# Gated mix of an S4 convolution and a gated linear unit: three sums of a table on GpSimd in halves, their factors and h in PSUM

## The chip, the cores and the metric

One core of a Trainium2 chip runs the whole program. The metric is device time of one execution, in microseconds (us); the figure for a kernel is the median of its runs. The engines are TensorE (PE, with its weight loads as PEld), VectorE (DVE), ScalarE (ACT), GpSimd (POOL) and SyncE (SP), which issues the DMAs here.

## The reference

With x of 2048 rows (time) and 512 channels, the output is `g * a + (1 - g) * b`:

```
g = sigmoid((x * gate_w).sum(-1))                 # one number a row
# a: S4 convolution, one kernel of 2048 taps a channel d, over 128 complex states n
P = exp(dt * A * l)                               # l = 0 .. 2047
K = einsum("dn,dnl,dn->dl", C, P, dt * B).real
a = irfft(rfft(x, 4096) * rfft(K, 4096))[:2048] + x * Dskip
# b: gated linear unit with 1792 hidden columns
b = (sigmoid(x @ w_gate) * (x @ w_up)) @ w_down
```

All of it is in float32.

## The kernel before

The convolution is done as a transform in two stages, with matmuls against constant matrices. `rows` (L382) transforms x in 16 pieces: load of a piece `u` (buffer tag `xs`, two buffers), four matmuls into two PSUM banks (L390), a copy of one bank by ACT (L391) and of the other by DVE (L392), and two DMAs to DRAM (`a_u`, L394).

`kgen` (L192) makes the taps K in 16 groups of 32 channels. The powers z^l of a state are built as a table `T` in three parts of 32 entries: T[:, 0] holds the small powers times the factor of the state, T[:, 1] powers with the step 32, T[:, 2] continues T[:, 1]. `bases` (L148) makes 11 powers z^(2^k) per group (`bz`) by Exp and Sin on ACT with DVE around it, in scratch tiles of tag `tmp`. `double` (L181) then makes twice as many entries out of those there are, as a complex product: two DVE products, L188 into a `tmp` tile and L189 into the table, and a DVE sum of both, L190. There are six doublings a group, of 64, 256, 512, 1024, 2048 and 2048 elements per partition. 128 small matmuls (L221) multiply the parts of the table and sum over the states into a bank of tag "kg"; ACT copies it (`kst`, L224, two buffers), 32 matmuls (L231) transform it into banks of tag "fft", and ACT puts it into `kev` (L235). T has one buffer: the table of the next group begins when the matmuls of L221 are through.

The gated unit (`glu`, L329) runs beside this. `load_x` (L330) loads half a stretch of x through the `xs` buffers and splits it into a rounded part and the rest. `weights` (L396) does the same with the weights of one block of 128 hidden columns, on DVE at L407 and L408 in the first half, from DRAM in the second. `hidden` (L416) makes 24 matmuls of 512 columns for a block, 12 into a bank for the gate and 12 into one for the up part (tag "gu", three banks). ACT takes the sigmoid (L431), DVE multiplies (`h`, L432), ACT rounds (`hh`, L433), DVE takes the rest (`hl`, L434). After three or four blocks the down products follow (L367, tag "dn", two banks) and a sum on DVE (L373).

After `kgen`, `finish` (L251) multiplies both transforms and goes back in 16 steps; `final` (L313) ends the transform and mixes. They take their banks from "fft" and "kg" as well, and the rest of the gated unit is spread between them.

The program is written in one order: the first table, 24 units of the gated unit, the rows with 32 units after each four, then after each half group 50 units (`run_b`; a unit is one matmul of 512 columns). A planner puts the instructions of each engine into a fixed order by their place in the program, when their inputs and buffers are there in its own account; what stands in `high_priority` (L215 to L239: from L221 to L238) goes first. Each engine works through its list in order, and so does SP with the DMAs. A bank or buffer goes to a new tile when the last reader of the old one is through. PSUM has eight banks: two of "fft", one of "kg", three of "gu" and two of "dn".

## Time and profile before

| | |
|---|---|
| median of 3 runs | 760.19 us (758.28 to 763.95) |
| the profiled execution's own time | 766.59 us |
| its span, first to last instruction | 764.7 us |
| busy share of PE, DVE, ACT, POOL | 93%, 81%, 50%, 0% |
| mean granted clock of TensorE | 0.966 |
| the chain that ended last | PE 44%, DVE 24%, ACT 14%, DMA 12% |

Busy time is the time in which an engine has an instruction in work; matmuls are pipelined, so a busy PE is not PE at its peak. The chain is followed back from the last instruction, at each step to what released it. A group's line has engine, operation, tiles out<-in, shapes and count, then busy us, mean ns of one, and idle time of the engine before them with what ended it. A wait's line has who waited for whom: us in total, times, and the longest.

### The profile page before, as it was taken

What the parts mean: (1) busy time and instruction counts of PE and PEld (TensorE: products, weight loads), DVE (VectorE), ACT (ScalarE), POOL (GpSimd) and SP (SyncE); (2) the same over time, 40 slices, a digit from 0 to 9 for tenths busy, and PEclk for the clock granted to TensorE, in tenths of its full rate; (3) what the DMA queues carried; (4) which work ended last, traced back from release to release, by engine and by line L of the source; (5) the groups of instructions that cost most, each with busy time, mean ns of one, the idle gap of its engine ahead of it and who ended that gap; (6) DMA issues with size and microseconds to landing.
All of it is one profiled execution on the core that took longest, in us unless ns stands there. A gap on an engine that the chain in (4) does not pass through costs nothing.

```text
span 764.7 us, 12698 instructions
## 1 busy us (share of the span) xinstructions
PE 709.3 (93%) x5024; PEld 478.7 (63%) x5024; DVE 622.5 (81%) x851; ACT 379.6 (50%) x624; POOL 3.6 (0%) x36
## 2 busy tenths in 40 slices
PE   5978869999999999999899998999999999999994
PEld 3445437787878778877687786877873333333640
DVE  5889796989998999998999898999927576477452
ACT  5264536381845446374565734637135655656310
POOL 0000000000000000000000000000000000000000
PEclk9789959999999999999999999999999999999998
DMA  6667652353134033655014330423167787876497
GB/s 230 185 201 215 171 158 77 128 188 132 63 110 140 34 132 109 220 172 188 12 34 157 122 150 8 138 96 99 56 244 255 266 264 240 266 249 227 143 308 249
DMA packets 63323, 123.03 MB, mean 161 GB/s; under 512 B 8480, under 2 KB 23072, under 8 KB 62240
## 3 DMA queue, kind: packets, MB, share of 16 engines
q1 hardware_dynamic: 63264, 122.23, 48.6%
q8 instruction: 39, 0.64, 0.3%
q14 instruction: 20, 0.16, 0.1%
HBM read 79.74 MB, written 42.47 MB: 160 GB/s over the span
## 4 chain that ended last, share of the span: by engine, by line
PE 44%; DVE 24%; ACT 14%; DMA 12%; issue 5%; SPq 1%; DVEq 0%; ACTq 0%
PE gups L424 13%; PE dps L367 11%; PE fps L247 8%; DVE T L189 5%; DVE T L190 5%; DVE tmp L188 4%; DMA wst<-wgu 4%; PE ips L280 4%; PE kps L221 3%; ACT L431 2%; PE fps L390 2%; DMA b_in<-b_s 2%; PE fps L231 2%; ACT gu L404 2%; DVE h L432 2%
## 5 line engine op out<-in xcount | busy, mean ns | idle before, releaser
L424 PE MATMUL gups<-xh,gu 128*128 128x512 f32 x896 | 294.5, 404 | 12.7 <-ACT gu L404 10.3
L424 PEld LDWEIGHTS gups<-xh,gu 128*128 128x128 f32 x896 | 170.6, 192 | 66.0 <-issue 12.9
L424 PE MATMUL gups<-xl,gu 128*128 128x512 f32 x448 | 181.3, 405 | 0.0
L367 PE MATMUL dps<-dnw,hh 128*128 128x512 f32 x448 | 152.9, 406 | 11.2 <-ACT hh L433 11.2
L188 DVE TENSOR_TENSOR tmp<-T,bz 128x64 f32<-128x64 f32 (+2 forms) x96 | 114.8, 1196 | 2.4
L190 DVE TENSOR_TENSOR T<-T,tmp 128x64 f32<-128x64 f32 (+2 forms) x96 | 114.7, 1195 | 0.8
L367 PEld LDWEIGHTS dps<-dnw,hh 128*128 128x128 f32 x448 | 84.3, 191 | 49.6 <-ACT hh L433 16.9
L189 DVE TENSOR_TENSOR T<-T,bz 128x64 f32<-128x64 f32 (+2 forms) x96 | 114.7, 1195 | 0.0
L424 PEld LDWEIGHTS gups<-xl,gu 128*128 128x128 f32 x448 | 86.2, 192 | 28.2 <-issue 10.5
L367 PE MATMUL dps<-dnw,hl 128*128 128x512 f32 x224 | 90.1, 404 | 2.1 <-DVE hl L434 1.3
L433 ACT ACTIVATE hh<-h 128x512 fp32r<-128x512 f32 x56 | 35.1, 628 | 70.1 <-DVE h L432 70.1
L431 ACT ACTIVATE sg<-gups 128x512 f32<-128x512 f32 x56 | 33.4, 596 | 50.5 <-PE gups L424 50.1
L367 PEld LDWEIGHTS dps<-dnw,hl 128*128 128x128 f32 x224 | 42.9, 192 | 15.8 <-issue 4.2
L432 DVE TENSOR_TENSOR h<-gups,sg 128x512 f32<-128x512 f32 x56 | 38.2, 685 | 16.9 <-PE gups L424 14.3
L404 ACT ACTIVATE gu<-wst 128x1024 fp32r<-128x1024 f32 x28 | 29.6, 1058 | 41.8 <-DMA wst<-wgu 29.2
L267 DVE TENSOR_TENSOR t<-fps,uf 128x512 f32<-128x512 f32 x32 | 22.0, 687 | 31.2 <-PE fps L247 19.8
L434 DVE TENSOR_TENSOR hl<-h,hh 128x512 fp32r<-128x512 f32 x56 | 38.4, 687 | 9.4 <-ACT hh L433 9.2
L247 PE MATMUL fps<-ak,w_in 128*64 128x512 f32 x128 | 42.1, 610 | 0.1
L235 ACT ACTIVATE kev<-fps 128x256 f32<-128x256 f32 x64 | 33.7, 675 | 15.3 <-PE fps L231 15.3
L247 PE MATMUL fps<-au,w_in 128*64 128x512 f32 x128 | 38.4, 610 | 1.9 <-DVE ud L301 0.8
L373 DVE TENSOR_TENSOR acc<-acc,dps 128x512 f32<-128x512 f32 x48 | 32.2, 682 | 7.8 <-PE dps L367 7.7
L221 PEld LDWEIGHTS kps<-T 128*32 128x32 f32 x2048 | 31.6, 115 | 8.8 <-issue 8.8
(84 smaller groups left out, 691.1 us busy)
## 6 DMA issues: line engine op xcount, KB each, us to landing
wst<-wgu SPq DMA_DIRECT2D x28, 512.0 KB, 4.4
a_u<-evu SPq DMA_DIRECT2D x32, 256.0 KB, 3.3
a_k<-kev SPq DMA_DIRECT2D x8, 1024.0 KB, 6.1
au<-a_u SPq DMA_DIRECT2D x16, 512.0 KB, 5.6
ak<-a_k SPq DMA_DIRECT2D x16, 512.0 KB, 5.0
b_s<-evb SPq DMA_DIRECT2D x32, 256.0 KB, 2.5
b_in<-b_s SPq DMA_DIRECT2D x16, 512.0 KB, 4.7
wsd<-wdn SPq DMA_DIRECT2D x28, 256.0 KB, 3.3
```

The source lines that it names most:

```text
L188: nc.vector.tensor_tensor(t2, src, sb, op=OP.mult)
L189: nc.vector.tensor_tensor(dst, src, br, op=OP.mult)
L190: nc.vector.tensor_tensor(dst, dst, t2[:, :, ::-1], op=OP.add)
L221: mm(p[32 * j:32 * j + 32, s].rearrange("p (a b) -> p a b", a=2), T[:, 0, ch, c], T[:, 1:3, ch, c], start=(c == 0), stop=(c == 1), tile_po ...
L247: mm(p[64 * kb:64 * kb + 64], w[:, kb, 64 * c:64 * c + 64], a(kb), start=True, stop=True, tile_position=(0, 64 * kb), skip_group_check=True)
L367: mm(p, a[:, hs], dnw[:, b], start=(n == 0), stop=(n == last))
L404: nc.scalar.activation(gu[:, 0], s4, AF.Copy)
L424: mm(p, gu[:, a, k, dc], b[:, dc], start=(n == 0), stop=(n == 11))
L431: nc.scalar.activation(sg, pp[0], AF.Sigmoid)
L432: nc.vector.tensor_tensor(h, pp[1], sg, op=OP.mult)
L433: nc.scalar.activation(hh, h, AF.Copy)
L434: nc.vector.tensor_tensor(hl, h, hh.bitcast(F32), op=OP.subtract)
```

## The change

- The sum of the doublings of 1024, 2048 and 2048 elements goes from DVE to GpSimd. Each of these doublings is cut into two calls of `double`: the first two by the parts T[:, 1] and T[:, 0], in this order, the last by its channels, 16 and 16. The scratch tiles have 1024 elements instead of 2048, and there are four instead of two; `bases` takes three tiles instead of one.
- The five powers that these doublings multiply by (and their negatives) are copied by ACT into a PSUM bank `kz`, from which DVE's products read them.
- `h` has no tile in SBUF: DVE's product is written over the up part, in its bank of tag "gu", where ACT and DVE read it.
- `kz` takes a PSUM bank, and the two of "fft" become one "f0". Where a second bank was used, it is "kg" (`rows`, `kgen`) or the one of `kz` (`stage2`, `final`).

```diff
--- before.py
+++ after.py
@@ -35,6 +35,7 @@
 NG = 16
 KS = [6, 0, 7, 1, 8, 2, 9, 3, 10, 4, 5]
 NB = len(KS)
+NZ = 6
 GROUPS = [4, 4, 3, 3]
 HALF = L // 2
 LN2H, LN2L = 0.693145751953125, 1.42860682030941723212e-6
@@ -97,8 +98,8 @@
     bp = ctx.enter_context(pool("bp"))
     ps = ctx.enter_context(pool("ps", 1, PSUM))
 
-    def fps(tag="fft", bufs=2):
-        return ps.tile([P, 512], F32, tag=tag, bufs=bufs, name="fps")
+    def fps(tag):
+        return ps.tile([P, 512], F32, tag=tag, name="fps")
 
 
     wu = cst.tile([P, 2, P], F32, name="wu")
@@ -143,7 +144,7 @@
 
 
     def tmp(pp):
-        return pp.tile([P, 2048], F32, tag="tmp", bufs=2, name="tmp")
+        return pp.tile([P, 1024], F32, tag="tmp", bufs=4, name="tmp")
 
     def bases(pp, gi):
 
@@ -155,10 +156,9 @@
         aa = pp.tile([P, 2, 32], F32, name="aa")
         nc.vector.tensor_tensor(aa, pg[:, 0:2], dg, op=OP.mult)
         sh = [P, 2, NB, 32]
-        t = tmp(pp)
         m = NB * 32
-        th, sc = (t[:, 2 * m * a:2 * m * (a + 1)].rearrange("p (c k b) -> p c k b", c=2, k=NB) for a in range(2))
-        af = t[:, 4 * m:5 * m].rearrange("p (k b) -> p k b", k=NB)
+        th, sc = (tmp(pp)[:, :2 * m].rearrange("p (c k b) -> p c k b", c=2, k=NB) for _ in range(2))
+        af = tmp(pp)[:, :m].rearrange("p (k b) -> p k b", k=NB)
         n = af.bitcast(I32)
         nc.vector.tensor_tensor(th, aa[:, :, None, :].to_broadcast(sh), pw[:, :, :, None].to_broadcast(sh), op=OP.mult)
         nc.scalar.activation(n, th[:, 1], AF.Copy)
@@ -178,16 +178,15 @@
         nc.vector.tensor_tensor(w[:, 1], w[:, 2], cb(1), op=OP.mult)
         return bz, w
 
-    def double(pp, dst, src, bz, k, nd, e):
+    def double(pp, dst, src, b, nd, e, add):
 
         sh = [P, nd, 2, e]
-        b = bz[:, :, k:k + nd // 32].rearrange("p u k b -> p u (k b)")
         t2 = tmp(pp)[:, :2 * nd * e].rearrange("p (d c e) -> p d c e", c=2, d=nd)
         br = b[:, 0, :, None, None].to_broadcast(sh)
         sb = b[:, 1:3].rearrange("p u d -> p d u")[:, :, :, None].to_broadcast(sh)
         nc.vector.tensor_tensor(t2, src, sb, op=OP.mult)
         nc.vector.tensor_tensor(dst, src, br, op=OP.mult)
-        nc.vector.tensor_tensor(dst, dst, t2[:, :, ::-1], op=OP.add)
+        add.tensor_tensor(dst, dst, t2[:, :, ::-1], op=OP.add)
 
     def kgen(pp):
         nxt = bases(pp, 0)
@@ -203,15 +202,24 @@
             nc.gpsimd.memset(T[:, 1, :, 0, 0:1], 1.0)
             nc.gpsimd.memset(T[:, 1, :, 1, 0:1], 0.0)
             nc.scalar.activation(T[:, 1, :, :, 1].rearrange("p d c -> p c d"), bz[:, 0:2, 1], AF.Copy)
-            double(pp, T[:, 0, :, :, 1:2], T[:, 0, :, :, 0:1], bz, 0, 32, 1)
+
+            kz = ps.tile([P, 3, NB - NZ, 32], F32, tag="kz", name="kz")
+            nc.scalar.activation(kz, bz[:, :, NZ:], AF.Copy)
+            double(pp, T[:, 0, :, :, 1:2], T[:, 0, :, :, 0:1], bz[:, :, 0], 32, 1, nc.vector)
             T2 = T[:, 0:2].rearrange("p t d c e -> p (t d) c e")
             for k in range(1, 5):
                 e = 2 ** k
-                double(pp, T2[:, :, :, e:2 * e], T2[:, :, :, 0:e], bz, 2 * k, 64, e)
+                if 2 * k < NZ:
+                    b = bz[:, :, 2 * k:2 * k + 2].rearrange("p u k b -> p u (k b)")
+                    double(pp, T2[:, :, :, e:2 * e], T2[:, :, :, 0:e], b, 64, e, nc.vector)
+                else:
+                    for t in (1, 0):
+                        double(pp, T[:, t, :, :, e:2 * e], T[:, t, :, :, 0:e], kz[:, :, 2 * k + t - NZ], 32, e, nc.gpsimd)
             yield 1
             if gi + 1 < NG:
                 nxt = bases(pp, gi + 1)
-            double(pp, T[:, 2], T[:, 1], bz, 10, 32, 32)
+            for d in (slice(0, 16), slice(16, 32)):
+                double(pp, T[:, 2, d], T[:, 1, d], kz[:, :, 10 - NZ, d], 16, 32, nc.gpsimd)
             hp = tc.high_priority(); hp.__enter__()
             p = ps.tile([P, 8, 64], F32, tag="kg", name="kps")
             for s in range(8):
@@ -225,7 +233,7 @@
 
             kv = [k[:, :, 32 * s4:32 * s4 + 32].rearrange("p k (j s) -> p s j k", j=4) for k in kev]
             for s in range(0, 8, 4):
-                p = fps()
+                p = fps("f0" if s == 0 else "kg")
                 for i in range(4):
                     for c in range(2):
                         mm(p[64 * c:64 * c + 64, P * i:P * i + P], kst[:, s + i], wk[:, c], start=True, stop=True,
@@ -242,7 +250,7 @@
 
     def stage2(a, w, done):
         for c in range(2):
-            p = fps()
+            p = fps(("f0", "kz")[c])
             for kb in range(2):
                 mm(p[64 * kb:64 * kb + 64], w[:, kb, 64 * c:64 * c + 64], a(kb), start=True, stop=True,
                    tile_position=(0, 64 * kb), skip_group_check=True)
@@ -314,7 +322,7 @@
 
         b = pp.tile([P, 2, D], F32, tag="big", bufs=3, name="b_in")
         nc.sync.dma_start(b, b_s[8 * m:8 * m + 8].rearrange("(j r) k d -> (r k) j d", j=2))
-        p = fps()
+        p = fps(("f0", "kz")[m % 2])
         for j in range(2):
             mm(p[64 * j:64 * j + 64], wf, b[:, j], start=True, stop=True, tile_position=(0, 64 * j),
                skip_group_check=True)
@@ -384,7 +392,7 @@
         u = bp.tile([P, D], F32, tag="xs", bufs=2, name="u")
         nc.sync.dma_start(u, xp[t])
         ev = pp.tile([P, 2, D], F32, tag="kev", bufs=2, name="evu")
-        ph = [fps(), fps()]
+        ph = [fps("f0"), fps("kg")]
         for jp in range(2):
             r = slice(64 * jp, 64 * jp + 64)
             mm(ph[jp], wu[r, jp], u[r], start=True, stop=True, tile_position=(64 * jp, 0))
@@ -425,7 +433,7 @@
                     n += 1
             pp.append(p)
         sg = bp.tile([P, 512], F32, tag="sg", bufs=2, name="sg")
-        h = bp.tile([P, 512], F32, tag="h", bufs=2, name="h")
+        h = pp[1]
         hh = bp.tile([P, 512], F32R, tag="hh", bufs=4, name="hh")
         hl = bp.tile([P, 512], F32R, tag="hl", bufs=4, name="hl")
         nc.scalar.activation(sg, pp[0], AF.Sigmoid)
```

## The prediction

> **What bounds the kernel now.** I begin with the page: the busy shares, then the slices, where a stage with another limit shows, and then the same figures by stage.
>
> ```profile
> PE 709.3 (93%) x5024; PEld 478.7 (63%) x5024; DVE 622.5 (81%) x851; ACT 379.6 (50%) x624; POOL 3.6 (0%) x36
> PE   5978869999999999999899998999999999999994
> DVE  5889796989998999998999898999927576477452
> PEclk9789959999999999999999999999999999999998
> ...
> 25.00:110.00 85.00, 68.13 (x448) 38.74 (x446) 74.19 (x92) 34.63 (x54) 0.41 (x4) 0.80 0.66 192
> 110.00:125.00 15.00, 13.12 (x117) 9.97 (x120) 12.57 (x12) 10.20 (x18) 0.00 (x0) 0.73 0.35 104
> 125.00:555.00 430.00, 418.85 (x3748) 339.39 (x3737) 398.94 (x495) 225.63 (x349) 2.79 (x26) 1.00 0.33 111
> 555.00:725.00 170.00, 167.18 (x595) 71.37 (x593) 103.22 (x179) 91.23 (x177) 0.00 (x0) 1.00 0.72 240
> ```
>
> The last four rows are stretches of the span, with the busy time of PE, its weight loads, DVE, ACT and POOL, then granted clock, DMA share and GB/s. From 125 to 555 us PE is busy for 418.85 of 430 us, so 11.2 us at most can be won there, although DVE is at 93% as well. From 555 on DVE has room and the change touches little. The stretch with room is 25 to 110 us: PE is idle for 17 of 85 us and runs at a clock of 0.80, while DVE is 87% busy.
>
> What paces that stretch? The row transforms (`rows`) run there, beside the first tables of `kgen`. I read who waits in SP's queue from 0 to 125 us, and then the order of a few PE and ACT instructions.
>
> ```profile
> SPq L394 <- DVE evu L392: 28.7, 15, 5.2
> SPq L385 <- PE fps L390: 10.8, 5, 4.5
> SPq L335 <- DVE xl L337: 6.3, 4, 3.1
> ...
> 53.91 1.78 PE L221 MATMUL kps<-T 128*32 128x64 f32 x113 [0.31 <-DVE T L190]
> 103.59 2.08 PE L390 MATMUL fps<-u,wu 64*128 64x512 f32 x4 [2.96 <-DMA u<-xp]
> 106.32 1.98 PE L231 MATMUL fps<-wk,kst 128*64 128x128 f32 x16 [0.65 <-ACT evu L391]
> 124.41 1.81 PE L221 MATMUL kps<-T 128*32 128x64 f32 x113
> ...
> 58.03 0.60 ACT L224 ACTIVATE kst<-kps 128x512 f32<-128x512 f32 x1 [0.45 <-PE kps L221]
> ```
>
> SP waited 28.7 us, in 15 of 16 rows, for DVE's copy of a row (L392), which stands in DVE's queue among the table's instructions; behind it wait the loads of the next rows. The last row is transformed at 103.59, and the second half of x (L335), on the rows' own buffer tag `xs`, comes only after it. So the front is paced by DVE through SP. The other rows show an order that the change will meet: `kst` of the first table is ready at 58.6 us, yet L231, which only wants a bank of tag "fft", starts at 106.32, behind the last row. Banks of a tag went to the users in program order.
>
> **The change part by part.** The moved sums are those with 2048 elements (two per group) and 1024 (one); the products stay, cut in two.
>
> ```profile
> L190 DVE TENSOR_TENSOR T<-T,tmp 128x2048 f32<-128x2048 f32 x32 | 73.1, 2284 | 0.1
> L190 DVE TENSOR_TENSOR T<-T,tmp 128x1024 f32<-128x1024 f32 x16 | 19.5, 1219 | 0.1
> L188 DVE TENSOR_TENSOR tmp<-T,bz 128x512 f32<-128x512 f32 x16 | 11.0, 690 | 0.4
> L163 DVE TENSOR_TENSOR tmp<-aa,pw 128x704 f32<-128x704 f32 x16 | 14.1, 884 | 0.0
> L165 DVE TENSOR_TENSOR tmp<-tmp 128x352 f32<-128x352 f32 x16 | 8.3, 518 | 0.0
> L204 POOL MEMSET T<- 128x32 f32 x16 | 2.5, 159 | 0.0
> L519 POOL MEMSET const-bfloat16-1.0<- 128x1 bf16 x1 | 0.1, 101 | 0.0
> L268 DVE TENSOR_TENSOR t2f<-fps,uf 128x512 f32<-128x512 f32 x32 | 21.9, 683 | 1.5 <-ACT y L277 1.5
> L224 ACT ACTIVATE kst<-kps 128x512 f32<-128x512 f32 x16 | 9.5, 594 | 14.1 <-PE kps L221 14.1
> ```
>
> *DVE.* Removed: 73.1 + 19.5 = 92.6 us, 5.8 us a group. Added: a 2048 product cut in two costs 2 x 1219 - 2284 = 154 ns more, a 1024 one 2 x 690 - 1219 = 161 ns; six products a group, 0.9 us. Net 4.9 us a group, 78 us in all.
>
> *POOL.* No row shows an add there. Its memsets take 101 ns for 1 element and 159 for 32: 1.87 ns an element. One such stream gives 2.0 us for a half of 1024 and 1.05 for 512. The lower end is DVE's own 1.22 and 0.69 us; the upper, three streams one after the other (two read, one written), 5.8 and 3.0 us. I take 2.0, the nearest row: 2 x 1.05 + 4 x 2.0 = 10.1 us a group, of which one starts every 32.9 us (the kps at 124.41 and, thirteen later, 552.21 us). The Trainium skill (GPSIMD Engine Reference, Performance versus the Vector engine) has 4497 ns for such an add of 2048 and 2293 on DVE, which the 2284 here agrees with; a half would be an estimated 2.25 us by it, 11.2 us a group, and the sum below would stay.
>
> *Length of a table.* From the 1024 doubling on, DVE alone needs 3 x 1.22 + 6 x 2.28 = 17.3 us. With halves, DVE's products (1.38 us a half, then 2.44) and POOL's sums overlap: products of the next half run while POOL adds the last, POOL ends 2.0 us behind DVE's 12.5, at 14.5 us. With 5.8 us sums POOL is the chain, 30.4 us. The products wait in DVE's in-order queue for POOL's sums, and `h`, `hl` and `acc` stand behind them; at 2.0 us POOL is through before its sum is wanted. Of four half tiles `tmp`, `bases` now holds three until L172; a second half may wait 2 us then, which the other work of DVE covers.
>
> *Operands in PSUM.* L268 reads PSUM and takes 683 ns, as L188's 690 from SBUF: no cost. The copy into `kz` is one ACT instruction of 480 elements, by L224 0.6 us a group; it has the three small doublings to hide behind, else 9.6 us in all.
>
> *h in PSUM.* The DVE instruction writes over its own input's bank, which is then kept until `hl` (L434) has read it.
>
> ```profile
> 441.06 0.68 DVE L432 TENSOR_TENSOR h<-gups,sg 128x512 f32<-128x512 f32 x1
> 444.66 0.69 DVE L434 TENSOR_TENSOR hl<-h,hh 128x512 fp32r<-128x512 f32 x1 [1.78 <-ACT hh L433]
> ...
> ACT hh L433 <- DVE h L432: 49.2, 25, 4.5
> PE dps L367 <- ACT hh L433: 7.4, 9, 2.1
> ...
> 291.82 13.37 PE gups L424 x59
> 552.21 1.99 PE L221 MATMUL kps<-T 128*32 128x64 f32 x128
> ```
>
> Here that is 445.35 - 441.74 = 3.6 us longer. A matmul takes 13.37 / 59 = 0.227 us, a bank of twelve 2.72 us; with three banks of `gups`, the next use that must have this one is three groups, 8.2 us, away. The longest wait of 125 to 555 us gives 4.5 + 0.7 + 3.6 = 8.8 us. So it is covered, and 0.6 us x 25 = 15 us is the price if the long waits were the rule; I take 0, since DVE's queue gets shorter. A PSUM output is shown by no row; DVE's instructions of 512 elements lie between 682 and 749 ns, so at most 56 x 0.07 = 4 us of DVE.
>
> *The banks.* "fft" becomes "f0", and the second bank of a row is now "kg", where `kps` also goes. By the order seen at 106.32, the first `kps` then comes behind the sixteenth row, not at 53.91, and since T has one buffer, the second table waits too. DVE is rid of that work while the rows run: the second table and most of the third, some 3 x (2 x 2.28 + 1.22 + 0.69) = 19.4 and 12 us of the 74.19. What is late next is `kgen` itself: with rows over at about 88 us, the third `kps` falls at 88 + 2 x 23 = 134 instead of 124 us. PE has the gated unit's matmuls meanwhile, so this costs nothing unless the last table is late at 555 us.
>
> **The sum**, on the profiled execution (span 764.7, its own time 766.59, the median of the runs shown 760.19, so 6.4 below it). Front: SP's 28.7 us of waits are the most that can go; PE's 17 idle us and a little slow clock say 22. Half of SP's waits, rounded, is -15 (0 to -22). 125 to 555 us: the 7.4 us that PE waited for `hh`, which is late because `h` is: half, -4 (0 to -11). Rest 0. So -19: 745.7 span, 747.6 own time, and **741** on the median.
>
> **The rivals.** *One port.* POOL's adds and DVE's instructions with two SBUF inputs could shut each other out. Those left are seven of `bases` per group (0.88, 0.52 and the like) and, in the first half of the unit, the splittings L407 and L408, about 2 a group; L432, L434, the products and `acc` have one input in PSUM. If each waited for half an add, 1.0 us, DVE would need 398.94 / 13.07 = 30.5 - 4.9 + 9.2 = 34.8 us a group against 32.9: +1.9 x 13 = 25, less the front's 15: 770; with whole adds 43.9 - 32.9 = 11 x 13 = +143 at worst. It decides from 7.3 us of waits a group. For it: `bases` runs just beside the last doubling. Against: POOL is busy a third of the time. The Trainium skill (SBUF — State Buffer, Who interferes with whom) states just this lock, for a DVE instruction with two SBUF inputs against a GpSimd one that reads SBUF, and frees one with a single SBUF input; no run here shows it yet.
> *The rows are not DVE's.* They may be paced by PE's order and the two buffers of `xs` (SP also waits 10.8 us for L390). Then the front stays, only the 4 us go: 756.
> *POOL is slow.* At 5.8 us the table lasts 30.4 + 4 + 2 + 1.5 = 38 us with its small doublings, `kps` and the start of the next; +5 x 13 = 65, less 15: 810. It decides at about 4 us a half.
> *It does not do what it says*: the sums move by name, so only the front's order could fail: if `kps` still went ahead of the rows, the front would gain about the removed sums of 25 to 110 us, 4 x 2.3 + 2 x 1.2 = 12 us. This lies in the forecast.
>
> **How the numbers follow.** Forecast (725 to 752) 0.58; the rows' own pace 0.17; the port 0.20 (764 to 790, more with a small chance); slow POOL 0.05. The range 722 to 786 leaves out a part of the port's tail, slow POOL and a gain over 5%, together under 0.2; the forecast's own is 725 to 752. Faster by over 1% 0.58, within 1%, which is about what a measurement of this kernel can tell from no change, 0.17, slower 0.25.
>
> **What would show it.** POOL at 160 us of busy time, 96 adds near 2.0 and 1.05 us; DVE near 545 us; the first `kps` behind the last row, and that row before 92 us; SP's wait for L392 under half of 28.7; from there PE at 9 in every slice. Wrong: adds over 4 us, L163 or L172 drawn out while POOL adds, PE waiting for `hl` before L424, or rows that still end at 104 us.

## The result, and the profile after

The changed kernel takes 809.62 us in the median of four runs (807.13 to 813.66), against 761.72 us for the kernel before beside it. The ratio is 1.0627, with a 95% interval of 1.0582 to 1.0672: **6.3% slower**, 48 us. The forecast was 741 us and the range ended at 786.

The profiled execution took 807.13 us, with a span of 805.4. First the page of the kernel after: the busy times, and the slices of PE, POOL and the clock.

```profile
PE 718.4 (89%) x5024; PEld 476.9 (59%) x5024; DVE 591.9 (73%) x899; ACT 388.9 (48%) x639; POOL 203.4 (25%) x132
PE   4797499989889889889998998988999999999995
...
POOL 0320023324243244432443533433600000000000
PEclk9898589999999999998999999999999999999997
```

DVE has 30.6 us less to do than before (622.5), and PE has more idle time: span less busy time is 55.4 us before and 87.0 after. PE is also busy for 9.1 us longer with the same 5024 matmuls. Together that is the 40.7 us by which the span grew. (The medians are 48 us apart, because the profiled execution of the kernel before, 766.59 us, was longer than its median, and that of the kernel after was the fastest of its four.) In the slices the 8s of PE stand where POOL has its digits, from the ninth slice to the twenty-eighth.

The same figures by stage, as the prediction showed them for the kernel before (busy time of PE, its weight loads, DVE, ACT and POOL, then granted clock, DMA share and GB/s):

```profile
25.00:110.00 85.00, 62.26 (x340) 36.01 (x338) 39.48 (x64) 31.21 (x49) 12.29 (x8) 0.76 0.69 205
110.00:125.00 15.00, 14.92 (x65) 12.02 (x65) 14.59 (x17) 5.56 (x10) 7.42 (x4) 1.00 0.09 31
125.00:555.00 430.00, 389.80 (x3465) 308.12 (x3464) 372.47 (x528) 228.59 (x355) 168.52 (x105) 0.98 0.31 104
```

From 125 to 555 us PE was idle for 11.2 us before; now it is 430 - 389.80 = 40.2. This is 29.0 of the 31.6 us of new idle time. The stretch from 25 to 125 us, in which I forecast the gain, got worse by 4.1 us (18.75 idle before, 22.82 now), although DVE's work from 25 to 110 us went from 74.19 to 39.48. A clock of 0.98 in place of 1.00 would make PE's work in the long stretch longer by an estimated 0.02 x 430 = 8.6 us, about the 9.1 us of longer busy time; that it is the reason isn't shown.

Who waits? From the lists of waits of the whole span, first four rows of the kernel before, then those of the kernel after (who waited for whom: us in total, times, the longest):

```profile
PE kps L221 <- DVE T L190: 0.3, 1, 0.3
PE dps L367 <- DVE hl L434: 1.3, 2, 0.9
PE fps L390 <- DMA u<-xp: 3.8, 2, 3.0
DVE evu L392 <- PE fps L390: 4.5, 4, 2.5
...
PE kps L229 <- POOL T L189: 27.8, 19, 3.0
PE dps L375 <- DVE hl L442: 10.2, 8, 2.2
PE fps L398 <- DMA u<-xp: 17.3, 4, 6.5
DVE evu L400 <- PE fps L398: 26.9, 10, 7.4
SPq L402 <- DVE evu L400: 22.7, 14, 3.1
```

Before, the `kps` matmuls waited 0.3 us in all for the last sum of the table, which DVE made; now 27.8 us, for POOL's. The down products wait 10.2 us for `hl` (1.3 before). The last three rows belong to the front and are read further down.

The groups of DVE and POOL, by shape (busy us, mean ns of one, idle before and what ended it), with L172 of the kernel before as the first row:

```profile
L172 DVE TENSOR_TENSOR bz<-tmp 128x704 f32<-128x704 f32 x16 | 14.2, 889 | 4.1 <-ACT tmp L169 4.0
...
L189 POOL TENSOR_TENSOR T<-T,tmp 128x1024 f32<-128x1024 f32 x64 | 157.8, 2477 | 153.2 <-DVE T L188 152.8
L189 POOL TENSOR_TENSOR T<-T,tmp 128x512 f32<-128x512 f32 x32 | 41.7, 1317 | 140.4 <-DVE T L188 140.3
L187 DVE TENSOR_TENSOR tmp<-T,kz 128x1024 f32<-128x1024 f32 x64 | 77.6, 1213 | 7.7 <-POOL T L189 7.7
L440 DVE TENSOR_TENSOR gups<-gups,sg 128x512 f32<-128x512 f32 x56 | 38.6, 693 | 32.6 <-PE gups L432 28.8 <-ACT sg L439 1.8 <-issue 1.3
L163 DVE TENSOR_TENSOR tmp<-aa,pw 128x704 f32<-128x704 f32 x16 | 34.5, 2153 | 0.0
L172 DVE TENSOR_TENSOR bz<-tmp 128x704 f32<-128x704 f32 x16 | 25.5, 1596 | 8.3 <-ACT tmp L169 7.9
L415 DVE TENSOR_TENSOR gu<-wst,gu 128x1024 fp32r<-128x1024 f32 x14 | 20.6, 1475 | 3.2 <-ACT gu L412 3.2
L345 DVE TENSOR_TENSOR xl<-xs,xh 128x512 fp32r<-128x512 f32 x16 | 15.2, 963 | 13.8 <-ACT xh L344 13.8
L416 DVE TENSOR_TENSOR dnw<-wsd,dnw 128x512 fp32r<-128x512 f32 x14 | 14.3, 1021 | 1.9 <-ACT dnw L413 1.9
L157 DVE TENSOR_TENSOR aa<-pg,dt 128x64 f32<-128x64 f32 x16 | 6.8, 427 | 1.3 <-DMA dt<-dts 1.2
```

A half sum of 1024 takes POOL 2.48 us, one of 512 takes 1.32. The products with a factor from PSUM (L187) and `h` written to PSUM (L440) take what they took. But the six last groups, all of them DVE instructions with both inputs in SBUF, are drawn out. L163 took 884 ns before, L172 889, L415 1219, L345 688, L416 686, L157 219. (L165, which also has two, never ran beside one of POOL's sums and stayed at 517 ns.) The differences times the counts are 20.3 + 11.3 + 3.6 + 4.4 + 4.7 + 3.3 = 47.6 us of DVE, 3.0 us a group.

Two stretches of the timeline show both costs at work, with other rows left out. Start, duration, engine and line, with the idle time before in brackets:

```profile
268.12 2.38 POOL L189 TENSOR_TENSOR T<-T,tmp 128x1024 f32<-128x1024 f32 x1 [5.79 <-DVE T L188]
268.18 3.06 DVE L172 TENSOR_TENSOR bz<-tmp 128x704 f32<-128x704 f32 x1
271.16 1.21 DVE L187 TENSOR_TENSOR tmp<-T,kz 128x1024 f32<-128x1024 f32 x1
272.30 1.21 DVE L188 TENSOR_TENSOR T<-T,kz 128x1024 f32<-128x1024 f32 x1
273.58 2.37 POOL L189 TENSOR_TENSOR T<-T,tmp 128x1024 f32<-128x1024 f32 x1 [3.09 <-DVE T L188]
276.01 1.98 PE L229 MATMUL kps<-T 128*32 128x64 f32 x124 [1.76 <-POOL T L189]
...
288.44 4.76 POOL L189 TENSOR_TENSOR T<-T,tmp 128x1024 f32<-128x1024 f32 x2 [1.19 <-DVE T L188]
291.15 2.80 DVE L163 TENSOR_TENSOR tmp<-aa,pw 128x704 f32<-128x704 f32 x1
293.88 0.68 DVE L442 TENSOR_TENSOR hl<-gups,hh 128x512 fp32r<-128x512 f32 x1
294.61 0.50 PE L375 MATMUL dps<-dnw,hl 128*128 128x512 f32 x1 [1.72 <-DVE hl L442]
```

*The port.* L172 starts 0.06 us behind POOL's sum and ends at 271.24, 0.74 us after that sum is through (270.50); undisturbed it takes 0.89. L163 starts in the middle of POOL's pair of sums and ends at 293.95, 0.75 us after their end (293.20). So DVE's instruction stands still for as long as POOL adds. The other way round it is POOL that waits: where L172 had started first, at 299.74 us, the sum that began at 299.90 took 2.98 us. `hl` is queued right behind L163, and PE behind `hl`, 1.72 us.
*The end of the chain.* The last product ends at 273.51, POOL adds until 275.95, and PE, which has come to `kps` in its list, starts 124 of the 128 matmuls at 276.01. It had stood still for 1.76 us.

### The profile page after: what moved, and what is told of

Its sections match the earlier page's. It is cut to its first block, busy times and chain, and to the rows that moved or that the text cites. A ratio compares the mean times of both kernels' runs of the same rounds, so it can differ in the third digit from the quotient of the medians.

```text
span 805.4 us, 12874 instructions
## 1 busy us (share of the span) xinstructions
PE 718.4 (89%) x5024; PEld 476.9 (59%) x5024; DVE 591.9 (73%) x899; ACT 388.9 (48%) x639; POOL 203.4 (25%) x132
## 4 chain that ended last, share of the span: by engine, by line
PE 35%; DVE 26%; ACT 6%; POOL 5%; issue 4%; DMA 4%; SPq 0%; DVEq 0%; ACTq 0%
PE gups L432 11%; PE fps L255 8%; DVE tmp L187 7%; DVE T L188 6%; PE dps L375 6%; POOL T L189 5%; PE ips L288 4%; DVE tmp L163 3%; PE kps L229 3%; PE fps L327 2%; DVE gups L440 1%; ACT L166 1%; DVE T L189 1%; DVE bz L172 1%; DMA b_in<-b_s 1%
## 5 line engine op out<-in xcount | busy, mean ns | idle before, releaser
L432 PE MATMUL gups<-xh,gu 128*128 128x512 f32 x896 | 292.7, 401 | 10.2 <-ACT gu L412 8.9
L189 POOL TENSOR_TENSOR T<-T,tmp 128x1024 f32<-128x1024 f32 (+1 forms) x96 | 199.5, 2090 | 293.6 <-DVE T L188 293.2
L375 PE MATMUL dps<-dnw,hh 128*128 128x512 f32 x448 | 157.3, 414 | 7.5 <-ACT hh L441 6.2
L187 DVE TENSOR_TENSOR tmp<-T,kz 128x1024 f32<-128x1024 f32 (+1 forms) x96 | 99.5, 1036 | 8.1 <-POOL T L189 7.7
L375 PE MATMUL dps<-dnw,hl 128*128 128x512 f32 x224 | 92.8, 414 | 10.2 <-DVE hl L442 10.2
L188 DVE TENSOR_TENSOR T<-T,kz 128x1024 f32<-128x1024 f32 (+1 forms) x96 | 99.3, 1034 | 0.0
L441 ACT ACTIVATE hh<-gups 128x512 fp32r<-128x512 f32 x56 | 33.2, 593 | 63.9 <-DVE gups L440 63.7
L440 DVE TENSOR_TENSOR gups<-gups,sg 128x512 f32<-128x512 f32 x56 | 38.6, 693 | 32.6 <-PE gups L432 28.8
L229 PE MATMUL kps<-T 128*32 128x64 f32 x2048 | 37.1, 223 | 27.9 <-POOL T L189 27.8
L442 DVE TENSOR_TENSOR hl<-gups,hh 128x512 fp32r<-128x512 f32 x56 | 38.2, 684 | 12.3 <-ACT hh L441 12.2
L255 PE MATMUL fps<-ak,w_in 128*64 128x512 f32 x128 | 46.4, 612 | 0.0
L398 PE MATMUL fps<-u,wu 64*128 64x512 f32 x64 | 25.6, 832 | 20.7 <-DMA u<-xp 17.3
L381 DVE TENSOR_TENSOR acc<-acc,dps 128x512 f32<-128x512 f32 x48 | 31.7, 680 | 14.4 <-PE dps L375 14.2
```

What stands on the lines that cost most here:

```text
L187: nc.vector.tensor_tensor(t2, src, sb, op=OP.mult)
L188: nc.vector.tensor_tensor(dst, src, br, op=OP.mult)
L189: add.tensor_tensor(dst, dst, t2[:, :, ::-1], op=OP.add)
L229: mm(p[32 * j:32 * j + 32, s].rearrange("p (a b) -> p a b", a=2), T[:, 0, ch, c], T[:, 1:3, ch, c], start=(c == 0), stop=(c == 1), tile_po ...
L255: mm(p[64 * kb:64 * kb + 64], w[:, kb, 64 * c:64 * c + 64], a(kb), start=True, stop=True, tile_position=(0, 64 * kb), skip_group_check=True)
L375: mm(p, a[:, hs], dnw[:, b], start=(n == 0), stop=(n == last))
```

## Experiments

Each kernel ran beside the kernel before; the ratio has its 95% interval. Two columns come from the profile of each: the idle time of PE from 25 to 125 and from 125 to 555 us (the stretch less PE's busy time in it), and PE's wait at `kps` for the table's last sum. The kernel before took 761.72 to 765.09 us beside these kernels, so between kernels that ran at different times a difference of 3 us means nothing.

| kernel | median us | ratio | PE idle 25–125 / 125–555 | `kps` waits |
|---|---|---|---|---|
| before | 761.72 | | 18.8 / 11.2 | 0.3 |
| after | 809.62 | 1.0627 (1.0582 to 1.0672) | 22.8 / 40.2 | 27.8 |
| e1_banks | 775.69 | 1.0175 (1.0137 to 1.0214) | 25.0 / 21.4 | 6.6 |
| e2_dve_sums | 804.49 | 1.0545 (1.0494 to 1.0597) | 25.1 / 29.8 | 11.6 |
| e3_last_dve | 784.03 | 1.0278 (1.0239 to 1.0317) | 25.0 / 22.2 | 6.7 |
| e4_h_sbuf | 808.79 | 1.0602 (1.0549 to 1.0655) | 23.3 / 43.0 | 29.9 |
| e5_rows_dn | 809.63 | 1.0620 (1.0553 to 1.0686) | 28.0 / 37.2 | 35.0 |
| e6_bases_first | 798.02 | 1.0446 (1.0376 to 1.0516) | 32.9 / 26.1 | 21.8 |
| e7_bases_first_last_dve | 784.61 | 1.0281 (1.0216 to 1.0346) | 30.8 / 14.2 | 7.4 |
| e8_pw_psum | 791.19 | 1.0360 (1.0302 to 1.0418) | 23.2 / 30.4 | 27.2 |
| e9_pw_last_dve | 771.59 | 1.0092 (1.0059 to 1.0125) | 25.2 / 10.6 | 4.4 |
| e10_pw_last_banks | 776.86 | 1.0152 (1.0126 to 1.0178) | 30.3 / 3.6 | 8.4 |
| e11_t0_only | 785.69 | 1.0273 (1.0240 to 1.0306) | 19.2 / 16.6 | 3.6 |
| e12_plain | 886.14 | 1.1616 (1.1552 to 1.1680) | 34.6 / 69.4 | 54.7 |
| e13_no_hp | 810.48 | 1.0628 (1.0564 to 1.0691) | 25.0 / 39.5 | 30.8 |
| e14_quarters | 798.98 | 1.0477 (1.0415 to 1.0538) | 23.3 / 24.5 | 15.2 |
| e15_second_half_dve | 786.69 | 1.0336 (1.0284 to 1.0388) | 26.2 / 24.1 | 19.8 |

The theory from this profile: the loss is PE's, at two places, `kps` behind POOL's last sum and `dps` behind a DVE instruction that POOL locks out. The rivals: the banks, `h` in PSUM, or DVE itself.

### The banks alone, and all sums back on DVE

e1 is the kernel before with nothing but the new banks.

```diff
-                p = fps()
+                p = fps("f0" if s == 0 else "kg")
...
-        ph = [fps(), fps()]
+        ph = [fps("f0"), fps("kg")]
```

> The kernel before with the change of banks alone: the rows take f0 and kg, kgen f0 and kg, finish and final f0 and a second bank; sums, powers and h stay as before. If the banks are the cause (the first table's matmuls behind all rows, kgen 45 us late from there), the time is near that of the changed kernel, 795 to 812 us, with the first kps near 103 us. If POOL's sums are the cause (PE stands before kps until they end), or h in PSUM, or the shared port, it is 755 to 772 us, since PE has the gated unit's matmuls to do while kgen is late.

Measured: 775.69 us, +13.6, between the two ranges: the banks are a part of the loss, not the whole. The first `kps` starts at 101.4 us instead of 53.9. The stretch that pays is shown by two rows of its windows:

```profile
25.00:110.00 85.00, 60.55 (x338) 35.73 (x338) 43.59 (x61) 30.08 (x47) 0.21 (x2) 0.82 0.67 198
125.00:555.00 430.00, 408.57 (x3746) 330.05 (x3745) 418.39 (x518) 232.20 (x361) 3.09 (x28) 1.00 0.32 109
```

DVE is busy for 43.59 us of the first 85 (74.19 before) and for 418.39 of the 430 (398.94 before). So the tables that no longer fit in between the rows are made later, where DVE was at 93% and is now at 97%. PE's idle time about doubles there, and it isn't won back in the front.

e2 is the kernel after with DVE in POOL's place.

```diff
-                        double(pp, T[:, t, :, :, e:2 * e], T[:, t, :, :, 0:e], kz[:, :, 2 * k + t - NZ], 32, e, nc.gpsimd)
+                        double(pp, T[:, t, :, :, e:2 * e], T[:, t, :, :, 0:e], kz[:, :, 2 * k + t - NZ], 32, e, nc.vector)
...
-                double(pp, T[:, 2, d], T[:, 1, d], kz[:, :, 10 - NZ, d], 16, 32, nc.gpsimd)
+                double(pp, T[:, 2, d], T[:, 1, d], kz[:, :, 10 - NZ, d], 16, 32, nc.vector)
```

> The changed kernel with all three sums back on DVE, still in halves, with the powers and h in PSUM and the changed banks. If POOL's part is the cause (its 2.5 us sums at the end of a table, or its hold on the port), the time falls to 765 to 780 us, what stays being the split products and sums, some 1.3 us of DVE a group, and L163 is back at 0.88 us. If banks or h in PSUM are the cause, it stays at 800 us or more.

Measured: 804.49 us, a miss, although L163 is back at 880 ns. Moving the sums to POOL, with all else of the change in place, costs only 5 us more, and the two intervals overlap. Read with e3, this is not "nothing happens" but a gain and a loss that cancel. So most of what the changed kernel loses, it loses with no sum on POOL as well: 13.6 us by the banks, and 28.8 us more than e1 with the halves, `h` and the powers in PSUM, and the smaller scratch tiles. DVE has 11.3 us more to do (631.8 us busy, e1 620.5). PE is idle for 10.6 us more (81.1 and 70.5) and busy for 19.7 us longer (722.1 and 702.4), at a mean clock of 0.947 against 0.967. The stretch from 125 to 555 us, and PE's largest wait in it:

```profile
125.00:555.00 430.00, 400.16 (x3506) 319.79 (x3505) 402.12 (x611) 221.49 (x351) 2.77 (x26) 0.96 0.32 108
PE dps L375 <- ACT hh L441: 13.6, 6, 4.1
```

In e1 the wait for `hh` is 2.1 us there. At the longest one, 4.08 us before 431.60 us, ACT was at L166 to L169 of `bases` from 426.60 on, and at `hh` only from 430.97 on. In stretches of 50 us from 125 to 525 us the clock was 1.00 where PE was busy for 47.1 us or more, and 0.90 to 0.97 where it was busy for 45.4 or less. No run takes these apart, so the cause of the 28.8 us stays open.

### The last doubling's sums back on DVE

```diff
             for d in (slice(0, 16), slice(16, 32)):
-                double(pp, T[:, 2, d], T[:, 1, d], kz[:, :, 10 - NZ, d], 16, 32, nc.gpsimd)
+                double(pp, T[:, 2, d], T[:, 1, d], kz[:, :, 10 - NZ, d], 16, 32, nc.vector)
```

> The changed kernel with the sums of the last doubling alone back on DVE, those of the 1024 and 2048 doublings before it stay on POOL. If the loss is PE waiting in its list before kps for POOL's last sum (some 28 us by the waits, 35 by the gaps), the wait of kps for POOL goes and the time is 770 to 785 us. If it is the port (48 us of drawn out DVE instructions, most of them beside the last doubling), about half of it stays and the time is 785 to 800 us. If banks or h in PSUM, 800 us or more.

Measured: 784.03 us, 25.6 less than after, in the range of the first of the three. PE's wait at `kps` goes from 27.8 to 6.7 us. In the groups, half of the lock is gone:

```profile
L163 DVE TENSOR_TENSOR tmp<-aa,pw 128x704 f32<-128x704 f32 x16 | 33.7, 2106 | 0.0
L172 DVE TENSOR_TENSOR bz<-tmp 128x704 f32<-128x704 f32 x16 | 14.2, 886 | 6.5 <-ACT tmp L169 6.5
```

L172, which ran beside the last doubling, is back at 886 ns. L163, beside the doubling before, is still at 2106. With e2 this gives the two halves of the move: the first two doublings on POOL are worth 804.49 - 784.03 = 20.5 us of gain, the last one 25.6 of loss. The loss has two parts that this edit removes together: DVE gets 38.9 us of sums and is busy for only 13.7 us longer (605.6 and 591.9), so 25 us of drawn-out instructions go with the wait at `kps`.

### h back in SBUF

```diff
-        h = pp[1]
+        h = bp.tile([P, 512], F32, tag="h", bufs=2, name="h")
```

> The changed kernel with h in its own SBUF tile again, so that the bank of the up part is free after the product. If the bank that is held is the cause, the time falls by 10 us or more, to below 800 us. If POOL's sums or the banks of kgen are, it stays at 803 to 816 us. If the port is what counts, hl now has two inputs in SBUF, is drawn out from 0.68 us to 1 us or more, and the time rises by 5 to 20 us.

Measured: 808.79 us, 0.8 less than after, within both intervals, as expected if the loss lies elsewhere. But `hl` is drawn out, as its third case has it:

```profile
L442 DVE TENSOR_TENSOR hl<-h,hh 128x512 fp32r<-128x512 f32 x56 | 51.5, 921 | 16.7 <-ACT hh L441 16.5
```

That is 921 ns in place of 684, 13.3 us in all, and of the 5 to 20 us forecast for it none shows in the time. Either such a lock can cost nothing at the end, or freeing the bank won as much; this run doesn't tell. `h` in PSUM neither costs nor gains on balance.

### Another bank for the rows; the bases first

e5 gives the rows' second piece a bank of "dn", so that "kg" is free for `kps`. e6 adds that the bases of the next group are made before the doublings, not beside the last. e7 is e6 with the last doubling's sums on DVE.

```diff
-        ph = [fps("f0"), fps("kg")]
+        ph = [fps("f0"), ps.tile([P, 512], F32, tag="dn", bufs=2, name="fps")]
```

In e6 and e7 also:

```diff
+            if gi + 1 < NG:
+                nxt = bases(pp, gi + 1)
             T2 = T[:, 0:2].rearrange("p t d c e -> p (t d) c e")
...
-            if gi + 1 < NG:
-                nxt = bases(pp, gi + 1)
```

> The changed kernel, but the second bank of a row is one of dn, so that kps has kg for itself and the first kps need not stand behind the rows. If the cost of the banks (13.6 us in the kernel before) adds to that of POOL, the first kps falls near 50 us and the time to 790 to 798 us. If PE's waits for POOL at the end of each table set the time alone, it stays at 803 to 812 us.

> As the one before (rows on dn), and the bases of the next group are made ahead of the doublings of a group instead of between the fourth and the last, so that their DVE instructions with two SBUF inputs do not stand beside POOL's sums. If the shared port is what costs (48 us of DVE in the changed kernel), L163 and L172 are back at 0.9 us, POOL's sums at 2.37 us, and the time falls by 15 us or more under that of the rows on dn alone, to 765 to 780 us. If PE's waits for POOL's last sum are what costs, they stay and the time is within 6 us of that of the rows on dn alone.

> As the one before, and the sums of the last doubling on DVE. If all three causes add (banks 14 us, port, kps waiting for POOL), this is the one without any of them, with 28 us less of DVE work than the kernel before and 22 us more for the halves: 752 to 764 us. If a part of the loss is yet another, such as h or the powers in PSUM, it stays at 770 us or more.

Measured: e5 809.63 us, as after and in its second range. The first `kps` does come at 50.0 us, but the second only at 120.0: the transform of `kst` also has its second half in "kg", and in program order that piece stands behind the first half, in "f0", which the rows hold (read from the order, not tested). e6 798.02, 11.6 less than e5 and between its two ranges. L172 is at 889 ns and L163 at 1296, against 1679 and 1663 in e5, and `kps` waits 21.8 us. e7 784.61: the port is nearly free (L163 886 ns, L172 927), `kps` waits 7.4 us, and PE's idle time from 125 to 555 us is down to 14.2. The expectation for e7 was missed all the same. Its idle time from 25 to 125 us is 30.8 (22.8 in after): in e5 to e7 the last row is transformed from 108.5, 115.6 and 113.3 us on, not from 99.3, and in e7 ACT stands for 6.9 us before a copy into `kz` among the rows, and PE for 8.8 us before the row that starts right behind it, at 84.73. From e6 to e7 the last doubling on POOL is worth 13.4 us, not 25.6, and again a part of it is lock: DVE gets 39.0 us of sums and is busy for 23.4 us longer.

### One operand of L163 in PSUM

The factors `pw` (22 numbers) are copied by ACT behind the powers in the bank of `kz`, and L163 reads them there. Its other input stays in SBUF, and the sums stay on POOL.

```diff
+            kzt = ps.tile([P, 512], F32, tag="kz", name="kz")
+            pwz = kzt[:, 480:502].rearrange("p (a b) -> p a b", a=2)
+            nc.scalar.activation(pwz, pw, AF.Copy)
...
-                nxt = bases(pp, gi + 1)
+                nxt = bases(pp, gi + 1, pwz)
```

> The changed kernel, with the 22 factors that L163 reads copied into the free columns of the bank of kz, so that L163 alone has one SBUF input instead of two; the work is the same. If it is the shared port that draws L163 out, its mean falls from 2.15 to 0.88 us while L172, left as it is, stays at 1.6 us; DVE loses 20 us of busy time and the time falls by 0 to 12 us. If it is something else (waiting for a scratch tile, POOL's writes), L163 stays near 2.1 us.

Measured: 791.19 us, 18.4 less than after. Its groups:

```profile
L172 DVE TENSOR_TENSOR bz<-tmp 128x704 f32<-128x704 f32 x16 | 21.9, 1367 | 7.8 <-ACT tmp L169 7.8
...
L163 DVE TENSOR_TENSOR tmp<-aa,kz 128x704 f32<-128x704 f32 x15 | 13.2, 879 | 0.0
```

L163 takes 879 ns in place of 2153, while L172 beside it, left with two SBUF inputs, is still drawn out. PE's wait for `hl` at `dps` falls from 10.2 to 1.3 us, and the wait at `kps` stays (27.2). This is the cleanest of the runs: but for a copy of 22 numbers a group, no work moved between engines, L172 stayed locked, and POOL's sums and the wait at `kps` are as they were. So the port by this one instruction is worth 18 us, more than the 0 to 12 expected: the 20 us that it cost DVE (16 x 1.27) came out nearly whole at the end. Of the 16.5 us by which the span is shorter, 10.2 are idle time of PE and 6.3 shorter busy time.

### Both cures together, and then the banks

e9 is e8 with the last doubling's sums on DVE. e10 adds the rows' bank of "dn" and both halves of `kst`'s transform in "f0", so that "kg" is for `kps` alone. e11 is e10 with only the sums of T[:, 0] left on POOL.

```diff
-                p = fps("f0" if s == 0 else "kg")
+                p = fps("f0")
...
-        ph = [fps("f0"), fps("kg")]
+        ph = [fps("f0"), ps.tile([P, 512], F32, tag="dn", bufs=2, name="fps")]
```

In e11 also:

```diff
-                        double(pp, T[:, t, :, :, e:2 * e], T[:, t, :, :, 0:e], kz[:, :, 2 * k + t - NZ], 32, e, nc.gpsimd)
+                        double(pp, T[:, t, :, :, e:2 * e], T[:, t, :, :, 0:e], kz[:, :, 2 * k + t - NZ], 32, e, nc.vector if t else nc.gpsimd)
```

> The changed kernel with both single cures that helped: the factors of L163 read from the bank of kz (18 us), and the sums of the last doubling on DVE (26 us). If the port and PE's wait before kps are two separate costs, most of both is won: 766 to 778 us. If the second cure worked because it also took POOL's sums away from beside L163, the gains overlap: 780 to 786 us.

> As the one before, and the banks mended: the second bank of a row is one of dn, both halves of the transform of kst go to f0, so that kps has kg alone as it had in the kernel before. The earlier try with dn alone left the second kps at 120 us, since the transform of the first kst held a place in the order of kg. If the late start of the tables costs what it cost in the kernel before (13.6 us), the first three kps are near 50, 85 and 120 us and the time falls by 6 to 14 us, to 758 to 770 us. If the rows on dn cost the gated unit what the tables win, it is unchanged within 5 us.

> As the one before, but POOL keeps only the sums of the part T[:, 0] in the 1024 and 2048 doublings, which no later doubling waits for; all others are on DVE. DVE gets 28 us of sums back, POOL falls from 120 to 60 us. If DVE's work is what counts from here, the time rises by 10 to 30 us. If POOL's place in the chain of the table and the port count more, it falls by 3 to 12 us.

Measured: e9 771.59 us, 38 less than after, as expected for two separate costs; e3 and e8 alone give 25.6 and 18.4, so 38 of 44 us add up. The rows of e9 from 25 to 125 and from 125 to 555 us:

```profile
25.00:125.00 100.00, 74.84 (x390) 44.90 (x389) 56.78 (x83) 37.01 (x59) 15.61 (x10) 0.82 0.61 179
125.00:555.00 430.00, 419.41 (x3761) 334.61 (x3760) 391.14 (x592) 239.29 (x389) 107.45 (x84) 0.99 0.34 111
```

In the long stretch PE is as busy as before (419.41 and 418.85). What is left, 0.9%, shows in the front: 25.2 us of idle time instead of 18.8. This is the best variant of the study, and it isn't faster than the kernel before.

e10 was to mend the front, and is slower than e9: 776.86 us, outside both of its ranges. The early tables do come (`kps` at 51.3 and 85.1 us), and the stretch from 125 to 555 us is the best of all, 3.6 us idle. But the last row falls to 114.75 us, and PE is idle for 30.3 us from 25 to 125, at a clock of 0.72 there (e9: 0.82). In idle time of the whole span the two balance (57.4 us, e9 58.2); what e10 has more is busy time of PE, 717.7 us against 711.9. What an early table wins behind the rows it loses among them. e11 is 9 us slower than e10, a little less than the 10 to 30 expected if DVE's work counts: POOL's busy time falls from 122.0 to 63.1 us, and DVE's rises from 596.0 to 620.2. Fewer sums on POOL is not better either.

### The sums alone

e12 is the kernel before with only the sums in halves on POOL: powers and `h` in SBUF, old banks.

```diff
-                double(pp, T2[:, :, :, e:2 * e], T2[:, :, :, 0:e], bz, 2 * k, 64, e)
...
+                    for t in (1, 0):
+                        double(pp, T[:, t, :, :, e:2 * e], T[:, t, :, :, 0:e], bz[:, :, 2 * k + t], 32, e, nc.gpsimd)
...
-            double(pp, T[:, 2], T[:, 1], bz, 10, 32, 32)
+            for d in (slice(0, 16), slice(16, 32)):
+                double(pp, T[:, 2, d], T[:, 1, d], bz[:, :, 10, d], 16, 32, nc.gpsimd)
```

> The kernel before with nothing but the sums on POOL, in halves: banks as before, powers and h in SBUF. If the port rule holds for the products too, DVE's products with two SBUF inputs (L188, L189 here) are drawn out beside POOL's sums, well over 1.21 us in the mean, and the time is above that of the changed kernel, 815 to 870 us. If the banks were the larger cost, it is below 800 us, and the first kps stands near 50 us.

Measured: 886.14 us, 16% slower than before, beyond the upper range, with the first `kps` at 51.9 us. Its groups:

```profile
L187 DVE TENSOR_TENSOR T<-T,bz 128x1024 f32<-128x1024 f32 x64 | 105.5, 1655 | 0.0
L186 DVE TENSOR_TENSOR tmp<-T,bz 128x1024 f32<-128x1024 f32 x64 | 97.6, 1525 | 23.0 <-POOL T L188 23.0
...
L188 POOL TENSOR_TENSOR T<-T,tmp 128x512 f32<-128x512 f32 x32 | 58.8, 1838 | 145.9 <-DVE T L187 145.9
```

The products now have two inputs in SBUF and take 1655 and 1525 ns instead of 1213, the sums of 512 on POOL 1838 instead of 1317, and `kps` waits 54.7 us. The two placements in PSUM, with the banks that they take, are thus worth 76 us to the change. They don't make it pay; they keep it from costing twice as much. (e4, which moves `h` alone back, changed nothing, so it should be the powers; they were not moved by themselves.)

### When PE stands at kps

e13 leaves out `high_priority`, so that PE's list might come to `kps` later. e14 cuts the last doubling into four pieces, so that the last sum is shorter. e15 is e8 with only the second half's sum of the last doubling on DVE.

```diff
-            hp = tc.high_priority(); hp.__enter__()
...
-            hp.__exit__(None, None, None)
```

The edits of e14 and of e15:

```diff
-            for d in (slice(0, 16), slice(16, 32)):
-                double(pp, T[:, 2, d], T[:, 1, d], kz[:, :, 10 - NZ, d], 16, 32, nc.gpsimd)
+            for d in (slice(0, 8), slice(8, 16), slice(16, 24), slice(24, 32)):
+                double(pp, T[:, 2, d], T[:, 1, d], kz[:, :, 10 - NZ, d], 8, 32, nc.gpsimd)
```

```diff
-            for d in (slice(0, 16), slice(16, 32)):
-                double(pp, T[:, 2, d], T[:, 1, d], kz[:, :, 10 - NZ, d], 16, 32, nc.gpsimd)
+            for d, add in ((slice(0, 16), nc.gpsimd), (slice(16, 32), nc.vector)):
+                double(pp, T[:, 2, d], T[:, 1, d], kz[:, :, 10 - NZ, d], 16, 32, add)
```

> The changed kernel without the high priority of kps and what follows it, so that PE's list has more of the gated unit's matmuls ahead of kps. No work moves between engines. If PE standing before kps for POOL's last sum costs time by itself, the gap before kps (34.8 us in all) shrinks below 15 us and the time falls by 10 us or more. If the table as a whole is late (its chain, not PE's place in it), the gap shrinks but the tables come later still and the time is 805 us or more.

> The changed kernel with the last doubling cut into four pieces of 512 elements instead of two of 1024: POOL's last sum then ends 1.3 us behind DVE's last product instead of 2.5 us, while DVE pays 16 x 4 x 0.15 = 10 us more for the cuts. If POOL's tail behind the last product is what PE waits for, the gap before kps falls by a third or more, and the time by 0 to 12 us. If POOL's order of sums (those of T[:, 0] before those of the last doubling) is what PE waits for, gap and time stay or rise by up to 12 us.

> The changed kernel with the factors of L163 in the bank of kz, and with the sum of the second half alone of the last doubling on DVE, so that the last instruction before kps is DVE's 1.21 us and not POOL's 2.5 us. DVE has 19 us less work than with both halves on DVE (771.6 us). If it is only the tail before kps that had to leave POOL, the time is 762 to 770 us. If POOL's earlier sums hold kps as well, it is 772 to 785 us.

Measured: e13 810.48 us, with `kps` waiting 30.8 us: no change, so that neither of its two conditions held. The priority is not what puts PE there too early; what does stays open. e14 798.98 us, 10.6 less than after and as expected, with nearly half of the wait gone:

```profile
PE kps L229 <- POOL T L189: 15.2, 28, 2.6
```

POOL's last piece is 1.32 us there instead of 2.48; 16 groups of 1.16 us are 18.6, of which 12.6 show as a shorter wait. But L172 falls with it, from 1596 to 1025 ns, so e14 is no test of the wait alone. e15 786.69 us, above both of its ranges, isn't told apart from e8 (791.19; the intervals overlap) and is slower than e9 (771.59); `kps` still waits 19.8 us for POOL's one sum of the last doubling. So the wait shrinks with the time that POOL ends behind DVE, and of these runs only those with the whole last doubling on DVE are rid of it. What the wait costs without the lock, no run shows: each edit that shortens it takes a part of the lock away as well.

## Why the prediction was wrong, by its steps

**The front, -15: failed.** The prediction put SP's 28.7 us of waits down to DVE's load, and so expected the last row before 92 us. DVE's load went (39.48 of 85 us), the first `kps` moved to 103.33 us, behind the rows, as forecast, and still SP waited 22.7 us for the copy. It wasn't the queue ahead of the copy: DVE itself waited 26.9 us for PE's row matmuls, and these 17.3 us for the load of `u` (3.8 before). The timeline of the kernel after shows the ring, with the rows of other work left out:

```profile
81.03 6.31 SPq L393 DMA_DIRECT2D u<-xp  x3
84.90 2.08 PE L398 MATMUL fps<-u,wu 64*128 64x512 f32 x4 [6.05 <-DMA u<-xp]
87.08 0.69 DVE L400 COPY evu<-fps 128x512 f32<-128x512 f32 x1 [7.44 <-PE fps L398]
...
87.83 7.05 SPq L402 DMA_DIRECT2D a_u<-evu  x6
...
94.97 0.63 SPq L393 DMA_DIRECT2D u<-xp  x1
...
99.32 2.08 PE L398 MATMUL fps<-u,wu 64*128 64x512 f32 x4 [6.52 <-DMA u<-xp]
```

Loads of `u` stand in SP's list behind the stores of earlier rows, which stand behind their copies. PE waits for a load for 6 us, then DVE for PE. DVE was rid of 34.7 us of work there, and the ring hardly got shorter. (Its order is read from the trace; no run took it apart.) The last row starts at 99.32 us against 103.59. In place of -15, the front has 4.1 us more of idle time. The rival "the rows are not DVE's" had this right, with 0.17.

**The banks: direction right, price wrong.** "Costs nothing unless the last table is late at 555" was the step; the last `kps` of after begins at 581.5 us, of e1 at 560.8, of before at 552.2, and e1 puts the price at 13.6 us, where the sum had 0. That it can't simply be mended (e5, e10) wasn't foreseen.

**125 to 555 us, -4: the step that decides.** It came out at +29.0 us of PE's idle time. The gain that it counted on did come: PE's wait for `hh` in this stretch fell from 7.4 to 2.4 us. The new waits outweighed it. Two sentences failed. "At 2.0 us POOL is through before its sum is wanted" failed at the last sum: I asked whether DVE's next product waits for POOL (7.7 us, little), not what PE, whose list has `kps` next, loses while it is POOL that ends the chain. PE lost 27.8 us there; with the lock that goes with it, the last doubling on POOL costs 13.4 (e6 to e7) to 25.6 us (e3). And "I take 0" for the waits of `h` and `hl`, "since DVE's queue gets shorter": the queue got shorter on average, but `hl` stands behind an L163 of 2.15 us. (For the bank that `h` holds, the working found 8.8 us of need against 8.2 of room and called it covered. In the trace PE waited for it once, for 1.1 us.)

**The port: mechanism right, its price judged by the wrong measure.** The rival named L163 and L172, half an add each, and 1.0 us for each wait; the means grew by 1.27 and 0.71 us, and all together by 3.0 us a group, under the 9.2 it was priced with. It said that it decides only from 7.3 us of waits a group, when DVE would be full. It costs far below that, where PE's instructions wait behind the blocked one: e8 took 18 us out with one operand, at 1.27 us a group. Not every such microsecond is paid, as e4 shows. The Trainium skill (SBUF — State Buffer, Who interferes with whom) describes such a lock between GpSimd and a DVE instruction with two SBUF inputs, and its absence with one. The trace and e8 agree: 2153 ns with two, 879 with one.

**POOL's sums.** Forecast 2.0 and 1.05 us, measured 2.48 and 1.32, 199.5 us in all instead of 160. It lies within the bounds, and at most 0.48 x 16 = 8 us of the wait at `kps` hangs on the size. Undisturbed ones here take 2.37 us. The Trainium skill (GPSIMD Engine Reference, Performance versus the Vector engine) has 4497 ns for an add of 2048 elements, by which a half would be an estimated 2.25 us; the trace has 0.12 us more.

**DVE near 545 us.** It is 591.9. The difference, 47, is the 47.6 us of the drawn-out instructions.

**What no term holds.** The sum gave the halves 0.9 us of DVE a group and the operands in PSUM nothing. e2 has both, with no sum on POOL, and is 28.8 us above e1. Step by step the 48 us are 13.6 for the banks (e1), 28.8 for this (e2), 20.5 of gain for the first two doublings on POOL (e3) and 25.6 of loss for the last. Which part of the change makes the 28.8 stays open. One wait that the working left out is ACT's own: its copy into `kz` waits for DVE's last product on the old bank, 13.8 us in all in after, and what ACT has next waits behind it.

**Right:** operands in PSUM at no cost for the instruction itself (1213 ns against 1219), that nothing waits for the copy into `kz` in the waits of after, a PSUM output at no cost (693 ns against 685), and that the second and third table move behind the rows.

The forecast's sum held a gain at each place and a zero at each new dependency. Of the "wrong" signs that the prediction listed, L163 and L172 are drawn out, PE waits for `hl` (mainly at the down products, not before L424's matmuls), and the last row ends at 101.4 us, nearer to 104 than to 92.

## What to carry to other kernels

When work moves to a second engine, ask first who waits at the end of the chain: if an engine with a fixed order does, it stands still while the helper ends later, whatever the busy shares say (27.8 us here, for two sums of 2.48 us a group). A busy share of 87% on the relieved engine, as in the front, is no proof that it paces a stage: look at what its own instructions wait for before counting its relief as a gain. Run the rest of the change without the move as well: here it cost 42 us by itself (e2). Before an elementwise operation goes to GpSimd, list the DVE instructions with two SBUF inputs beside it and who is queued behind them; one operand in PSUM took 18 us out.

## What the runs showed of the hardware

- A DVE instruction with two SBUF inputs stood still until POOL's sum was through. Those of 128x704 elements shown above ended 0.74 and 0.75 us after it, and L163 took 2153 ns in the mean instead of 884. With one input in PSUM it took 879 ns beside the same sums.
- POOL pays too where DVE's products have two SBUF inputs: 1838 ns for a sum of 128x512 in e12, 1317 in the kernel after. A sum of 128x1024 that began behind a DVE instruction with two took 2.98 us instead of 2.37.
- A float32 sum of 128x1024 took POOL 2.37 us undisturbed, against 1.22 on DVE; 128x512 took 1.30 against 0.69.
- DVE writing its result over its own input in PSUM took 693 ns for 128x512, against 685 into SBUF.
